# An accumulator split into two tiles, and a last unit computed by halves of its activations

## The chip, the cores and the metric

The kernel runs on one core of a Trainium2 chip. The metric is the device time of one launch in microseconds (us). The core has a matrix engine (PE, TensorE; its weight loads are shown apart as PEld), a vector engine (DVE, VectorE), an activation engine (ACT, ScalarE), GpSimd (POOL) and SyncE (SP), whose queue issues nearly all DMAs here. Each engine works through its own list of instructions in order; between engines there are semaphores, which a framework sets from the tiles that instructions read and write. PE writes its results to PSUM; a bank in this text is a piece of it with 512 fp32 values in each partition, the output of one matmul of 128x512.

## What is computed

The reference chains three parts. A gated linear attention over 3072 tokens of 256 channels comes first; then a feed-forward part with token shift, whose output is gated; then a second feed-forward part:

```python
# first feed-forward part (weights 256x1024, 1024x256, 256x256)
xk = mu_k * x + (1 - mu_k) * x_prev
xr = mu_r * x + (1 - mu_r) * x_prev
k = np.maximum(xk @ w_k, 0.0)
v = k * k @ w_v
x = 1.0 / (1.0 + np.exp(-(xr @ w_r))) * v
# second feed-forward part (weights 256x2048, 2048x256)
h = x @ w_in
return (h - np.tanh(h)) @ w_out
```

The kernel evaluates h - tanh(h) by a polynomial where every |h| is small. It counts the sums of squares that lie under a bound, and only if that count falls short does a branch at the very end compute everything again with the exact function. With the inputs given here it doesn't.

## The kernel before, in words

Tokens are the columns. Both feed-forward parts work on six blocks (`j`) of 512 tokens, with the 256 channels as two halves of 128 partitions (`c`). Each fp32 product is made of three matmuls: the weights and the activations are split into a high and a low part, and high x high, low x high and high x low are added up. The first part takes 4 units (`i`) of 256 hidden channels per block, the second 8 units, 48 in all. A unit has an up product into a pair of banks (`product`, lines 755 to 758), elementwise work on ACT and DVE, and a down product (`down_part`, lines 760 to 767: for each `c` three matmuls of 128x512) into the accumulator.

The accumulator `acc` (line 223) is one tile of two banks, `acc[:, c]` for channel half `c`. It has one buffer. In the first part, when a block's down products are all in, `final` (line 816) multiplies the whole of it by the gate on DVE, one operation of 128x1024, into `xall`. In the second part two copies (`out_copy`, line 910), one for each `c`, take it to SBUF, and SP stores them. Only then can the down products of the next block begin. Attention takes 12 groups of 256 tokens, which are interleaved with the first feed-forward part up to about 165 us; weights are decoded on the way. PE also writes `acc` in the prologue: matmuls on zeros that fill waiting time, and one small product (lines 217, 562, 659 to 666).

The order of the instructions of each engine isn't written out by hand. `Plan` (line 108) is a list scheduler that runs when the program is built: each step is a task with an estimated time on one or two possible engines (`t_dve(n)` is (n + 145)/960 us, `t_act` the same for ACT), with what it comes after, a rank, and the buffers (`Ring`) that it takes. `run` always issues the task that can start first by these estimates, by rank where several can, and chooses the engine where a task may run on two. `final` is such a task, with `t_dve(1024)` = 1.218 us. The real start is set by the semaphores, not by the estimates.

The last of the 48 units has its elementwise work cut into two halves (`x`, the two blocks of 128 hidden channels), so that each operation is 128x512: square with its sum (`poly_a`), `poly_b`, `poly_c`, `g_high`, `g_low`. Behind the plan, `count` (line 955) compares the 49 columns of sums with the bound on DVE, adds them up over the partitions with a matmul into `pv`, and writes `flag`. Then `last_unit` (line 962) does the last down products in three parts of the output: (`c` 0, 512 columns), (`c` 1, first 256), (`c` 1, last 256), each over both halves of the activations, 18 matmuls; it loads `flag` into registers of every engine, and copies the three parts with ACT, DVE, ACT in turn, with a store behind each. After that comes the branch over the second computation (line 1040).

Of the kernel before, what the change touches and what calls it, by code (L numbers as in the profile page):

```python
# [69 lines left out]
def t_act(n, more=0.0):  # L70
    return 0.172 + n / 1200 + more


def t_dve(n):
    return (n + 145) / 960
# [32 lines left out]
class Plan:  # L108
# [10 lines left out]
    def add(self, on, fn, after=(), rank=0.0, takes=(), uses=(), port=False, dma=0.0, func=None):  # L119
        t = Task()  # L120
        t.on, t.fn, t.rank, t.takes, t.port, t.dma, t.func, t.end = on, fn, rank, takes, port, dma, func, None
        t.after = [x for x in after if x is not None]
        for ring, key in (*takes, *uses):
            ring.use(key, t)
        self.tasks.append(t)
        return t
# [69 lines left out]
def chain_kernel(ctx, tc, xb, a, an, a0, bc, mu_k, mu_r, w_k, w_v, w_r, w_in, w_out, out):  # L196
# [17 lines left out]
    def fill(n):  # L214

        for _ in range(n):
            PE.matmul(acc[:, 0], quiet, quiet.unsqueeze(1).to_broadcast([P, NC4, P]), start=True, stop=True)

    def bank(name, shape=(2, BLK)):
        return pairs.tile([P, *shape], F32, tag="pair", name=name)  # L220


    acc = accp.tile([P, 2, BLK], F32, name="acc")


    WORK = dict(xh=2, xl=2, l=3, h=3, f=3, s=2)
# [23 lines left out]
    def block(j, o):  # L250

        c, n = col(j * BLK) + o, col(j * BLK + GT) - col(j * BLK)
        return xall[:, :, c:c + 2 * n].rearrange("p c (h s) -> p c h s", s=n)[..., 0:GT]

    def halves(t):
        return t.rearrange("p c (h s) -> p c h s", s=GT)
# [294 lines left out]
    def prologue(fetch1):  # L551
# [7 lines left out]

        def warm(n):  # L560
            for _ in range(n):
                PE.matmul(acc[:, 0], quiet, quiet.unsqueeze(1).to_broadcast([P, NC4, P]), start=True, stop=True)

        def load(t, v):
            return lambda: nc.sync.dma_start(out=t, in_=v)
# [92 lines left out]

        def t_dec():

            ps = acc[:, 1]
            for i in range(2):
                PE.matmul(ps[:, 0:NU], tri, las[:, i], start=i == 0, stop=i == 1)

        def t_dexp():
            A.activation(out=dec.rearrange("p g q c -> p (g q c)"), in_=acc[:, 1, 0:NU], func=AF.Exp)

        def t_nu():
            for nm in "kr":
# [90 lines left out]
    def down_part(wh, wl, hl, k, e, first, last):  # L760

        h, l = hl
        for c in range(2):
            cs = slice(c * P, (c + 1) * P)
            PE.matmul(acc[:, c], wh[:, k, cs], h[:, e], start=first, stop=False, skip_group_check=True)  # L765
            PE.matmul(acc[:, c], wl[:, k, cs], h[:, e], start=False, stop=False, skip_group_check=True)  # L766
            PE.matmul(acc[:, c], wh[:, k, cs], l[:, e], start=False, stop=last, skip_group_check=True)  # L767

    mixes, mixed, gate, prs, pks, kks, ksq = ({} for _ in range(7))

# [43 lines left out]
            V.tensor_tensor(out=kk, in0=kk, in1=kk, op=ALU.mult)  # L814

    def final(j):
        V.tensor_tensor(out=block(j, 0), in0=halves(acc), in1=halves(gate.pop(j)), op=ALU.mult)  # L817

    MM6 = 6 * 0.23

    def ffn1(X, wk, wr, wv):

        fin, began = {}, {}
        for j in range(NBLK):
            r0 = RANK_F0 + RANK_F * j
            need = [X.get(i) for i in range(2 * j - 1, 2 * j + 2)]
            mx = {}
            for nm, r in (("k", r0 - 3), ("r", r0 + RANK_R - 3)):
                x, fm = (R["x"], (nm, j)), (R["f"], (nm, j))
                m = add(dict(A=2 * t_act(BLK)), lambda e, nm=nm, j=j: mix(nm, j), [*need, began.get((j - 1, 1 if nm == "k" else NP - 1))], r - 0.1, [fm])  # L830
                m = add(dict(V=2 * t_dve(BLK)), lambda e, nm=nm, j=j: mix_ahead(nm, j), [m], r, (), [fm], port=True)
                h = add(dict(A=t_act(1024), V=t_dve2(1024)), lambda e, q=(nm, j): high(e, mixed, q, mixes[q], "xh"), [m], r, [x], [fm], port=True)
                mx[nm] = add(dict(V=t_dve(1024)), lambda e, q=(nm, j): low(mixed, q, mixes[q], "xl"), [h], r, (), [x, fm], port=True)
            p = mx["r"]
            for m in range(2):
                p = add(dict(P=MM6), lambda e, j=j, m=m: receptance(j, m), [p, wr], r0 + RANK_R, [] if m else [(R["pair"], ("pr", j)), (R["s"], ("rs", j))], [(R["x"], ("r", j))])
            rs = add(dict(A=t_act(1024)), lambda e, j=j: sigmoid(j), [p], r0 + RANK_R, (), [(R["pair"], ("pr", j)), (R["s"], ("rs", j))], func="sig")
            dn = None
            for i in range(NP):
                r = r0 + RANK_U * i  # L840
                pair, fk, l, h = ((R[x], ("k", j, i)) for x in ("pair", "f", "l", "h"))
                p = mx["k"]
                for e2 in range(2):
                    p = add(dict(P=MM6), lambda e, j=j, i=i, e2=e2: up(j, i, e2), [p, wk[i]], r, [] if e2 else [pair, fk], [(R["x"], ("k", j))])
                last_up = began[j, i] = p
                q = add(dict(A=t_act(1024), V=t_dve(1024)), lambda e, j=j, i=i: relu(j, i, e), [p], r, (), [pair, fk])
                q = add(dict(A=t_act(1024), V=t_dve(1024)), lambda e, j=j, i=i: square(j, i, e), [q], r, (), [fk], port=True)
                q = add(dict(A=t_act(1024), V=t_dve2(1024)), lambda e, q=(j, i): high(e, ksq, q, kks[q], "h"), [q], r, [h], [fk], port=True)
                q = add(dict(V=t_dve(1024)), lambda e, q=(j, i): low(ksq, q, kks[q], "l"), [q], r, [l], [fk, h], port=True)
                for e2 in range(2):  # L850
                    k = 2 * i + e2
                    dn = add(
                        dict(P=MM6), lambda e, j=j, i=i, e2=e2, k=k: down_part(wvh, wvl, ksq[j, i], k, e2, k == 0, k == 2 * NP - 1),
                        [q, dn, wv[i]], r + RANK_D, [] if k else [(R["acc"], ("f1", j))], [l, h],
                    )
            fin[j] = add(dict(V=t_dve(1024)), lambda e, j=j: final(j), [dn, rs], r0, (), [(R["acc"], ("f1", j)), (R["s"], ("rs", j))])
        return fin, last_up, mx["r"]


# [49 lines left out]

    def out_copy(j, c, e):  # L910
        ob = obs[j, c] = w2["ob"].tile([P, BLK], F32, tag="ob", bufs=3, name="ob")
        copy(e, ob, acc[:, c])

    def out_store(j, c):
        nc.sync.dma_start(out=out[c * P:(c + 1) * P, j * BLK:(j + 1) * BLK], in_=obs[j, c])
# [1 line left out]
    def ffn2(fin, last_up, last_mix, win, wout):  # L917
        ups, last_high = [last_mix] * 2, None
        for j in range(NBLK):
# [5 lines left out]
            for i in range(NP2):  # L925
# [9 lines left out]
                for x in range(2) if end else [0]:  # L935
                    sl = slice(x, x + 1) if end else ALL
                    w = BLK if end else 2 * BLK

                    q = add(dict(A=2 * t_act(w) + 0.2), lambda e, j=j, i=i, sl=sl, c=n + x: poly_a(j, i, sl, c), [p], r, (), [pair, s, fq])
                    q = add(dict(V=t_dve(w)), lambda e, j=j, i=i, sl=sl: poly_b(j, i, sl), [q], r, (), [s, fq], port=True)  # L940
                    q = add(dict(V=t_dve(w)), lambda e, j=j, i=i, sl=sl: poly_c(j, i, sl), [q], r, (), [pair, fq])
                    q = last_high = add(dict(A=t_act(w), V=t_dve2(w)), lambda e, j=j, i=i, sl=sl: g_high(j, i, sl, e), [q, last_high], r, [] if x else [h, l], [fq], port=True)
                    q = add(dict(V=t_dve(w)), lambda e, j=j, i=i, sl=sl: g_low(j, i, sl), [q], r, (), [l, h, fq], port=True)
                    gl.append(q)
                if end:
                    break
                for e2 in range(2):
# [4 lines left out]
                    q = add(dict(A=t_act(BLK), V=t_dve(BLK)), lambda e, j=j, c=c: out_copy(j, c, e), [dn], r, [ob], [(R["acc"], ("f2", j))])  # L952
                    add(dict(S=0.38), lambda e, j=j, c=c: out_store(j, c), [q], r, (), [ob], dma=0.7)

    def count():

        V.tensor_scalar(out=less, in0=sums, scalar1=T2, scalar2=0.0, op0=ALU.is_lt, op1=ALU.add, accum_out=w2["okc"])
        pv = bank("pv")
        PE.matmul(pv[0:1, 0, 0:1], w2["okc"], ones, start=True, stop=True)
        V.tensor_copy(flag, pv[0:1, 0, 0:1])  # L960

    def last_unit():

        j, i = NBLK - 1, NP2 - 1
        h, l = gs[j, i]
        parts = [(0, slice(0, BLK)), (1, slice(0, GT)), (1, slice(GT, BLK))]
        for c, t in parts:
            cs = slice(c * P, (c + 1) * P)
            for e in range(2):
                wh, wl = (w2["out" + x][i][:, e, cs] for x in "hl")  # L970
                for w, g in ((wh, h), (wl, h), (wh, l)):
                    PE.matmul(acc[:, c, t], w, g[:, e, t], start=False, stop=e == 1 and g is l, skip_group_check=True)
        below = nc.values_load(flag[0:1, 0:1], min_val=0, max_val=P * (NU2 + 1))
        for (c, t), e in zip(parts, "AVA"):
            ob = w2["ob"].tile([P, BLK], F32, tag="ob", bufs=3, name="ob")
            copy(e, ob[:, t], acc[:, c, t])
            nc.sync.dma_start(out=out[c * P:(c + 1) * P, j * BLK + t.start:j * BLK + t.stop], in_=ob[:, t])
        return below

# [26 lines left out]
    with tc.manual_schedule():  # L1006
# [26 lines left out]
            done2.append(decode(100 + n, lambda n=n: unit_jobs(n // 2)[n % 2], lambda: w2["ob"], "2", RANK_X0 + RANK_X * n, [op]))  # L1033
        ffn2(fin, last_up, last_mix, done2[0::2], done2[1::2])
        plan.run()
        count()
        below = last_unit()
        w1_stack.close()
        again = ctx.enter_context(tc.tile_pool(name="again", bufs=1))
# [65 lines left out]
```

## Time and profile before

| | us |
|---|---|
| median of 3 runs | 507.31 (507.01 to 508.74) |
| the profiled execution | 507.41 |
| its span, first to last instruction | 505.7 |

| engine | busy us | share of the span |
|---|---|---|
| PE | 482.5 | 95% |
| DVE | 401.4 | 79% |
| ACT | 293.1 | 58% |
| POOL | 6.1 | 1% |

A busy time is a sum of durations of single instructions. Matmuls overlap in the records: one of 128x512 is shown with some 0.39 us, but in a run of them one starts every 0.23 us. What PE loses is therefore read best from the starts: where two that follow one another are further apart than 0.23 us, PE waited.

### The profile page before, as it was taken

How to read it: one execution, taken by the hardware profiler on the slowest of the kernel's cores; microseconds unless marked ns; L12 is line 12 of the kernel's file. 1: busy time of each engine (PE TensorE's matmuls, PEld its weight loads, DVE VectorE, ACT ScalarE, POOL GpSimd, SP SyncE). 2: the span in 40 equal slices, each digit the busy share in tenths (PEclk: the TensorE clock that was granted, in tenths of full speed). 3: DMA queues.
4: the chain of work that ended last, by engine and by line, in shares of the span. 5: the costliest groups of instructions: out<-in, count | busy, mean ns of one | idle time of the engine just before them, and what ended most of it. 6: DMA issues, size and time to landing. Idle time of an engine off the chain costs nothing.

```text
span 505.7 us, 10270 instructions
## 1 busy us (share of the span) xinstructions
PE 482.5 (95%) x4462; PEld 382.3 (76%) x4462; DVE 401.4 (79%) x509; ACT 293.1 (58%) x374; POOL 6.1 (1%) x22
## 2 busy tenths in 40 slices
PE   5979989999999999999999999999999999999993
PEld 2557767888778878877788788788878888887882
DVE  6698998999669999996877868767876966787581
ACT  5366976775757666766464654645565454455551
POOL 4000000000000000000000000000000000000000
PEclk9789999999999999999999999999999999999998
DMA  6575455211022212210000100100010010001001
GB/s 196 183 231 181 136 156 152 76 47 34 1 86 84 83 43 84 83 43 0 1 0 1 41 0 1 41 3 0 1 41 0 1 41 1 0 1 41 0 2 47
DMA packets 14259, 27.40 MB, mean 54 GB/s; under 512 B 2392, under 2 KB 3288, under 8 KB 14208
## 3 DMA queue, kind: packets, MB, share of 16 engines
q1 hardware_dynamic: 14140, 26.66, 16.9%
q8 instruction: 37, 0.61, 0.5%
q14 instruction: 14, 0.11, 0.1%
q10 hardware_dynamic: 68, 0.02, 0.0%
HBM read 23.30 MB, written 3.34 MB: 53 GB/s over the span
## 4 chain that ended last, share of the span: by engine, by line
PE 69%; DVE 18%; ACT 6%; DMA 3%; issue 2%; ACTq 0%; POOL 0%; DVEq 0%; POOLq 0%; SPq 0%
PE acc L765 10%; PE acc L767 10%; PE acc L766 10%; PE ph L755 8%; PE ph L758 8%; PE ph L756 8%; PE pk L755 3%; PE pk L756 2%; PE pk L758 2%; DVE l L788 2%; DVE f L889 2%; DVE f L893 1%; DMA raw<-in_w_in 1%; PE py L504 1%; PE py L482 1%
## 5 line engine op out<-in xcount | busy, mean ns | idle before, releaser
L884 ACT ACTIVATE s<-ph 128x1024 f32<-128x1024 f32 (+1 forms) x49 | 49.4, 1009 | 76.3 <-PE ph L758 76.3
L889 DVE SCALAR_TENSOR_TENSOR f<-f,s 128x1024 f32<-128x1024 f32 (+1 forms) x49 | 58.8, 1200 | 34.8 <-ACT f L885 34.4
L755 PE MATMUL ph<-xh,winh 128*128 128x512 f32 x192 | 76.2, 397 | 0.0
L756 PE MATMUL ph<-xh,winl 128*128 128x512 f32 x192 | 75.5, 393 | 0.0
L765 PE MATMUL acc<-h,wouth 128*128 128x512 f32 x188 | 74.5, 396 | 0.2
L767 PE MATMUL acc<-l,wouth 128*128 128x512 f32 x188 | 74.5, 396 | 0.1
L766 PE MATMUL acc<-h,woutl 128*128 128x512 f32 x188 | 74.3, 395 | 0.0
L902 DVE TENSOR_TENSOR l<-f,h 128x1024 fp32r<-128x1024 f32 (+1 forms) x49 | 58.9, 1201 | 18.6 <-ACT h L352 18.0
L352 ACT ACTIVATE h<-f 128x1024 fp32r<-128x1024 f32 (+1 forms) x43 | 44.7, 1039 | 48.5 <-DVE f L893 45.6
L893 DVE TENSOR_TENSOR f<-ph,f 128x1024 f32<-128x1024 f32 (+1 forms) x49 | 58.9, 1201 | 3.3
L758 PE MATMUL ph<-xl,winh 128*128 128x512 f32 x192 | 60.2, 395 | 0.0
L885 ACT ACTIVATE f<-s,biases 128x1024 f32<-128x1024 f32 (+1 forms) x49 | 55.6, 1136 | 1.6
L765 PEld LDWEIGHTS acc<-h,wouth 128*128 128x128 f32 x188 | 35.4, 188 | 10.0 <-ACT f L885 1.4
L755 PEld LDWEIGHTS ph<-xh,winh 128*128 128x128 f32 x192 | 36.1, 188 | 8.8
L758 PEld LDWEIGHTS ph<-xl,winh 128*128 128x128 f32 x192 | 36.1, 188 | 8.6
L767 PEld LDWEIGHTS acc<-l,wouth 128*128 128x128 f32 x188 | 35.4, 188 | 9.2 <-DVE l L902 1.0
L756 PEld LDWEIGHTS ph<-xh,winl 128*128 128x128 f32 x192 | 36.1, 188 | 8.1
L766 PEld LDWEIGHTS acc<-h,woutl 128*128 128x128 f32 x188 | 35.4, 188 | 8.2
L755 PE MATMUL pk<-xh,wkh 128*128 128x512 f32 x96 | 39.3, 409 | 0.0
L765 PE MATMUL acc<-h,wvh 128*128 128x512 f32 x96 | 38.5, 401 | 0.9 <-DVE xall L817 0.9
L756 PE MATMUL pk<-xh,wkl 128*128 128x512 f32 x96 | 38.2, 398 | 0.0
L767 PE MATMUL acc<-l,wvh 128*128 128x512 f32 x96 | 37.6, 392 | 0.3 <-DVE l L788 0.3
(138 smaller groups left out, 754.0 us busy)
## 6 DMA issues: line engine op xcount, KB each, us to landing
bct<-in_bc SPq DMA_DIRECT2D x12, 384.0 KB
xbt<-in_xb SPq DMA_DIRECT2D x12, 384.0 KB
raw<-in_w_in SPq DMA_DIRECT2D x8, 512.0 KB
raw<-in_w_out SPq DMA_DIRECT2D x8, 512.0 KB
out<-ob SPq DMA_DIRECT2D x11, 256.0 KB
raw<-in_w_k SPq DMA_DIRECT2D x4, 512.0 KB
raw<-in_w_v SPq DMA_DIRECT2D x4, 512.0 KB
raw<-in_w_r SPq DMA_DIRECT2D x1, 512.0 KB
```

What stands on the lines that cost most here:

```text
L352: A.activation(out=out, in_=in_, func=AF.Copy)
L755: PE.matmul(o, wh[:, k, ms], hi[:, k], start=k == 0, stop=False)
L756: PE.matmul(o, wl[:, k, ms], hi[:, k], start=False, stop=False)
L758: PE.matmul(o, wh[:, k, ms], lo[:, k], start=False, stop=k == 1)
L765: PE.matmul(acc[:, c], wh[:, k, cs], h[:, e], start=first, stop=False, skip_group_check=True)
L766: PE.matmul(acc[:, c], wl[:, k, cs], h[:, e], start=False, stop=False, skip_group_check=True)
L767: PE.matmul(acc[:, c], wh[:, k, cs], l[:, e], start=False, stop=last, skip_group_check=True)
L884: A.activation(out=s, in_=phs[j, i][:, e], func=AF.Square, accum_out=sums[:, c:c + 1])
L885: A.activation(out=qs[j, i][:, e], in_=s, func=AF.Square, scale=PA, bias=pbias)
L889: V.scalar_tensor_tensor(out=q, in0=q, scalar=PG, in1=s, op0=ALU.add, op1=ALU.mult)
L893: V.tensor_tensor(out=q, in0=phs[j, i][:, e], in1=q, op=ALU.mult)
L902: V.tensor_tensor(out=l[:, e], in0=qs[j, i][:, e], in1=f(h[:, e]), op=ALU.subtract)
```

## The change

`acc` becomes two tiles of one bank, `accs[0]` and `accs[1]`, in the same pool; each use names its own. `final` becomes two operations of 128x512, and its estimate in the plan two times `t_dve(512)`, 1.369 us. Counting becomes a task of the plan, after the squares of the second half of the last unit, at a rank two below its neighbours. `last_unit` first issues the small matmul on the count, then the down products by halves of the activations: all of half 0 (both `c`), then all of half 1, 12 matmuls of 512 columns; the flag is converted behind them in the text. The last copies are `c` 0 whole on DVE, and `c` 1 by halves on ACT.

```diff
-    acc = accp.tile([P, 2, BLK], F32, name="acc")
+    accs = [accp.tile([P, BLK], F32, name=f"acc{c}") for c in range(2)]
...
-            PE.matmul(acc[:, c], wh[:, k, cs], h[:, e], start=first, stop=False, skip_group_check=True)
-            PE.matmul(acc[:, c], wl[:, k, cs], h[:, e], start=False, stop=False, skip_group_check=True)
-            PE.matmul(acc[:, c], wh[:, k, cs], l[:, e], start=False, stop=last, skip_group_check=True)
+            PE.matmul(accs[c], wh[:, k, cs], h[:, e], start=first, stop=False, skip_group_check=True)
+            PE.matmul(accs[c], wl[:, k, cs], h[:, e], start=False, stop=False, skip_group_check=True)
+            PE.matmul(accs[c], wh[:, k, cs], l[:, e], start=False, stop=last, skip_group_check=True)
...
     def final(j):
-        V.tensor_tensor(out=block(j, 0), in0=halves(acc), in1=halves(gate.pop(j)), op=ALU.mult)
+        o, g = block(j, 0), halves(gate.pop(j))
+        for c in range(2):
+            V.tensor_tensor(out=o[:, c], in0=accs[c].rearrange("p (h s) -> p h s", s=GT), in1=g[:, c], op=ALU.mult)
...
-            fin[j] = add(dict(V=t_dve(1024)), lambda e, j=j: final(j), ...
+            fin[j] = add(dict(V=2 * t_dve(BLK)), lambda e, j=j: final(j), ...
...
-        copy(e, ob, acc[:, c])
+        copy(e, ob, accs[c])
...
-                    q = add(dict(A=2 * t_act(w) + 0.2), lambda e, ...: poly_a(j, i, sl, c), ...
+                    q = polys = add(dict(A=2 * t_act(w) + 0.2), lambda e, ...: poly_a(j, i, sl, c), ...
...
+                    if x:
+                        add(dict(V=0.28), lambda e: counted(), [polys], r - 2)
...
-    def count():
+    def counted():

         V.tensor_scalar(out=less, in0=sums, scalar1=T2, scalar2=0.0, op0=ALU.is_lt, op1=ALU.add, accum_out=w2["okc"])
-        pv = bank("pv")
-        PE.matmul(pv[0:1, 0, 0:1], w2["okc"], ones, start=True, stop=True)
-        V.tensor_copy(flag, pv[0:1, 0, 0:1])

     def last_unit():

         j, i = NBLK - 1, NP2 - 1
         h, l = gs[j, i]
-        parts = [(0, slice(0, BLK)), (1, slice(0, GT)), (1, slice(GT, BLK))]
-        for c, t in parts:
-            cs = slice(c * P, (c + 1) * P)
-            for e in range(2):
+        pv = bank("pv")
+        PE.matmul(pv[0:1, 0, 0:1], w2["okc"], ones, start=True, stop=True)
+        for e in range(2):
+            for c in range(2):
+                cs = slice(c * P, (c + 1) * P)
                 wh, wl = (w2["out" + x][i][:, e, cs] for x in "hl")
                 for w, g in ((wh, h), (wl, h), (wh, l)):
-                    PE.matmul(acc[:, c, t], w, g[:, e, t], start=False, stop=e == 1 and g is l, skip_group_check=True)
+                    PE.matmul(accs[c], w, g[:, e], start=False, stop=e == 1 and g is l, skip_group_check=True)
+        V.tensor_copy(flag, pv[0:1, 0, 0:1])
         below = nc.values_load(flag[0:1, 0:1], min_val=0, max_val=P * (NU2 + 1))
-        for (c, t), e in zip(parts, "AVA"):
+        for c, e, t in ((0, "V", slice(0, BLK)), (1, "A", slice(0, GT)), (1, "A", slice(GT, BLK))):
             ob = w2["ob"].tile([P, BLK], F32, tag="ob", bufs=3, name="ob")
-            copy(e, ob[:, t], acc[:, c, t])
+            copy(e, ob[:, t], accs[c][:, t])
             nc.sync.dma_start(out=out[c * P:(c + 1) * P, j * BLK + t.start:j * BLK + t.stop], in_=ob[:, t])
         return below
...
         plan.run()
-        count()
         below = last_unit()
```

The remaining lines of the diff put `accs[0]` or `accs[1]` for `acc[:, 0]` or `acc[:, 1]` in the prologue.

## Rows read from the trace of the kernel before

**Rows 1.** Windows: span of each stretch, then each engine's busy time and count

```profile
core 0: us, PE busy (x) PEld busy (x) DVE busy (x) ACT busy (x) POOL busy (x), PEclk, DMA share, GB/s
85.00:165.00 80.00, 79.77 (x1259) 64.67 (x1246) 69.88 (x99) 54.30 (x66) 0.00 (x0) 1.00 0.20 60
165.00:235.00 70.00, 68.87 (x303) 56.19 (x302) 64.19 (x87) 44.29 (x53) 0.00 (x0) 1.00 0.20 61
235.00:494.00 259.00, 258.68 (x1107) 207.32 (x1105) 195.02 (x179) 137.55 (x177) 0.00 (x0) 1.00 0.03 11
```

**Rows 2.** Timeline, PE in the last unit: start us, us, what [idle before <-releaser]

```profile
493.74 0.39 PE L767 MATMUL acc<-l,wouth 128*128 128x512 f32 x1
495.00 0.19 PE L959 MATMUL pv<-ones,okc 128*1 128x1 f32 x2 [0.87 <-DVE less L957]
495.12 0.50 PE L972 MATMUL acc<-h,wouth 128*128 128x512 f32 x1
495.46 0.39 PE L972 MATMUL acc<-h,woutl 128*128 128x512 f32 x1
...
497.91 0.28 PE L972 MATMUL acc<-l,wouth 128*128 128x256 f32 x1
```

**Rows 3.** Timeline, ACT and DVE in the last unit, up to the count

```profile
493.26 1.48 DVE L902 TENSOR_TENSOR l<-f,h 128x512 fp32r<-128x512 f32 x2
493.37 0.63 ACT L352 ACTIVATE h<-f 128x512 fp32r<-128x512 f32 x1 [0.69 <-DVE f L893]
...
494.65 0.20 DVE L957 TENSOR_SCALAR_CACHE_REDUCE less<-sums 128x49 f32<-128x49 f32 x1
```

**Rows 4.** Timeline, the last copies and the three stores

```profile
498.23 0.60 ACT L352 ACTIVATE ob<-acc 128x512 f32<-128x512 f32 x1 [4.22 <-PE acc L972]
...
498.85 1.31 SPq L977 DMA_DIRECT2D out<-ob  x3
498.86 0.42 DVE L354 COPY ob<-acc 128x256 f32<-128x256 f32 x1 [3.48 <-ACT ob L352]
499.31 0.38 ACT L352 ACTIVATE ob<-acc 128x256 f32<-128x256 f32 x1 [0.49 <-DVE ob L354]
```

**Rows 5.** Instructions of line 1040: xcount, ns min/median/max, first and last start

```profile
L1040 SPq EVENT_SEMAPHORE  x8: 17/17/17, 503.3 to 503.8; - x8
...
L1040 PEldq COMPARE_BRANCH  x1: 3362/3362/3362, 496.0 to 496.0; - x1
...
L1040 SPq COMPARE_BRANCH  x1: 50/50/50, 500.2 to 500.2; - x1
```

**Rows 6.** Timeline, two block boundaries of the second part

```profile
279.48 1.29 DVE L354 COPY ob<-acc 128x512 f32<-128x512 f32 x2 [2.53 <-PE acc L767]
...
280.21 0.63 PE L758 MATMUL ph<-xl,winh 128*128 128x512 f32 x2
280.92 0.47 PE L765 MATMUL acc<-h,wouth 128*128 128x512 f32 x1
281.22 0.39 PE L766 MATMUL acc<-h,woutl 128*128 128x512 f32 x1
...
325.69 0.44 PE L765 MATMUL acc<-h,wouth 128*128 128x512 f32 x1
325.96 0.40 PE L766 MATMUL acc<-h,woutl 128*128 128x512 f32 x1
```

**Rows 7.** Timeline, the fourth block boundary of the first part

```profile
185.50 0.61 PE L758 MATMUL pk<-xl,wkh 128*128 128x512 f32 x2
185.61 1.22 DVE L817 TENSOR_TENSOR xall<-acc,s 128x1024 f32<-128x1024 f32 x1
...
186.98 0.47 PE L765 MATMUL acc<-h,wvh 128*128 128x512 f32 x1 [0.86 <-DVE xall L817]
```

**Rows 8.** Windows, two stretches while attention is still interleaved

```profile
72.00:74.00 2.00, 0.40 (x15) 0.31 (x15) 2.00 (x5) 0.67 (x1) 0.00 (x0) 1.00 0.09 25
74.00:76.00 2.00, 2.00 (x6) 1.57 (x7) 2.00 (x4) 1.58 (x2) 0.00 (x0) 0.56 0.79 208
```

More of the change, by code (lines that the diff above doesn't have):

```diff
@@ L216, in fill @@
         for _ in range(n):
-            PE.matmul(acc[:, 0], quiet, quiet.unsqueeze(1).to_broadcast([P, NC4, P]), start=True, stop=True)
+            PE.matmul(accs[0], quiet, quiet.unsqueeze(1).to_broadcast([P, NC4, P]), start=True, stop=True)
     def bank(name, shape=(2, BLK)):
         return pairs.tile([P, *shape], F32, tag="pair", name=name)
-    acc = accp.tile([P, 2, BLK], F32, name="acc")
+    accs = [accp.tile([P, BLK], F32, name=f"acc{c}") for c in range(2)]
     WORK = dict(xh=2, xl=2, l=3, h=3, f=3, s=2)
@@ L561, in warm @@
             for _ in range(n):
-                PE.matmul(acc[:, 0], quiet, quiet.unsqueeze(1).to_broadcast([P, NC4, P]), start=True, stop=True)
+                PE.matmul(accs[0], quiet, quiet.unsqueeze(1).to_broadcast([P, NC4, P]), start=True, stop=True)
         def load(t, v):
@@ L659, in t_dec @@
         def t_dec():
-            ps = acc[:, 1]
+            ps = accs[1]
             for i in range(2):
@@ L665, in t_dexp @@
         def t_dexp():
-            A.activation(out=dec.rearrange("p g q c -> p (g q c)"), in_=acc[:, 1, 0:NU], func=AF.Exp)
+            A.activation(out=dec.rearrange("p g q c -> p (g q c)"), in_=accs[1][:, 0:NU], func=AF.Exp)
         def t_nu():
@@ L855, in ffn1 @@
                     )
-            fin[j] = add(dict(V=t_dve(1024)), lambda e, j=j: final(j), [dn, rs], r0, (), [(R["acc"], ("f1", j)), (R["s"], ("rs", j))])
+            fin[j] = add(dict(V=2 * t_dve(BLK)), lambda e, j=j: final(j), [dn, rs], r0, (), [(R["acc"], ("f1", j)), (R["s"], ("rs", j))])
         return fin, last_up, mx["r"]
@@ L937, in ffn2 @@
                     w = BLK if end else 2 * BLK
-                    q = add(dict(A=2 * t_act(w) + 0.2), lambda e, j=j, i=i, sl=sl, c=n + x: poly_a(j, i, sl, c), [p], r, (), [pair, s, fq])
+                    q = polys = add(dict(A=2 * t_act(w) + 0.2), lambda e, j=j, i=i, sl=sl, c=n + x: poly_a(j, i, sl, c), [p], r, (), [pair, s, fq])
                     q = add(dict(V=t_dve(w)), lambda e, j=j, i=i, sl=sl: poly_b(j, i, sl), [q], r, (), [s, fq], port=True)
```

## The prediction

> **What bounds the kernel.** I read the windows first. From 85 to 494 us PE does nothing but its own work: it is busy for 79.77 of 80 us, 68.87 of 70 and 258.68 of 259, at the full clock, while DVE has 10.12, 5.8 and 64 us to spare [rows 1]. So in these 409 us only what makes PE start a matmul late costs time, and the changed kernel has the same columns to multiply. The other place is the end. PE's last matmul begins at 497.91 [rows 2], yet the span ends at 505.7: copies, stores and the end of the program stand one behind another there. Second I looked along PE's starts for gaps over 0.23 us (between 85 and 494 they are few), and third at the timeline of the last unit. One word on size: 0.3% of 507.31 is 1.5 us, about what a measurement of this kernel can tell from no change.
>
> **The last unit, PE.** PE has nothing to wait for until 493.74, the start of its last matmul in the plan; the next could start at 493.97. It starts at 495.00, and it is the one on the count: that matmul waits for DVE's comparison at 494.65 [rows 2, 3], which stands on DVE behind both `g_low`. In the changed kernel the comparison lies further up on DVE, and the matmul can go at 493.97: 1.03 us. The first down product follows 0.12 us later, as now, at 494.09. Now the second comes 0.34 after the first, as after any wait, against 0.23 in a run [rows 2]: another 0.11. The columns are the same, 6 x 512 and 12 x 256 against 12 x 512. The last of 12 then starts at 494.09 + 11 x 0.233 = 496.66 and takes 0.39: PE ends at 497.05 instead of 498.19, **1.14 us** earlier.
>
> Are the activations there? Half 0 is needed whole at the third matmul, 494.56; its low part is the first of two from 493.26, done by about 494.0. Half 1 is needed from 494.09 + 6 x 0.233 = 495.49, its low part at 495.96; they are done at 494.00 and 494.74 [rows 3]. The comparison, moved ahead of them on DVE, delays them by its 0.20 us at most: cover of 0.36, 1.29 and 1.02 us is left. If the comparison is put behind them by the plan, the first 1.03 us are not won. I don't expect it: its rank is two lower than that of the steps that become ready with it, and the list scheduler takes the lower. The conversion of the flag comes behind the last `g_low` on DVE, at about 494.95, and the load of the flag on SP still ends a microsecond before SP's first store. `last_unit`'s DVE copy stands behind it in the queue, with the same cover.
>
> **The last copies.** Now ACT reads `c` 0 from 498.23, when all 18 matmuls are done, though the matmuls of `c` 0 are the first six; DVE waits for ACT, ACT again for DVE [rows 4]. All three take turns, 498.23 to 499.69. In the changed kernel `c` 0 ends with the ninth of 12 matmuls: start 495.95, end 496.34. DVE's copy of 512 columns takes at most 0.7 (two take 1.29 [rows 6]): done at 497.05. ACT copies the halves of `c` 1 from 497.07, 0.38 each [rows 4]: done at 497.45 and 497.83. SP needs 1.31 us for three issues [rows 4], some 0.46 from one to the next, so the stores are issued at 497.08, 497.54 and 498.0; now they are at 498.85, 499.3 and 499.77. From there on nothing is changed: SP's branch at 500.2, and its first step behind it at 503.3 [rows 5]. The end is **1.77 us** earlier, PE's 1.14 among them.
>
> Rows 4 show that readers of two different banks take turns here. [...] By the rows alone, if they went on taking turns, it would be 1.2 us; that is a rival below.
>
> **The boundaries of blocks in the second part.** The first down product of a block needs the accumulator free of both copies. At 280.21 PE begins two matmuls, so the next is due at 280.68 and the one after it at 280.91; that one starts at 281.22, 0.31 late. Where ACT copies, at 325.69, the next is 0.27 behind, 0.04 late [rows 6]. There are three boundaries of the first kind and two of the second: 3 x 0.31 + 2 x 0.04 = **1.0 us**. With two tiles the copy of `c` 0 can start 0.70 us sooner (three matmuls of 0.233), and PE needs only `accs[0]` at first and `accs[1]` three matmuls later. Both are free by 280.2, with at least 0.5 us over: all of it goes, and PE, which bounds this stretch, keeps it.
>
> **The boundaries in the first part.** `final` of block 3 starts at 185.61 and PE, due at 185.97, starts at 186.98, some 0.15 behind its end [rows 7]. Its first half would be done at 186.30 and PE could start at 186.45: **0.5 us**. The second half is done by 187.0, before PE's fourth matmul at 187.15. At the other boundaries of this part PE has no gap to give back.
>
> **What it adds.** Two operations of half the size instead of one: 1.29 us for two copies of 512 columns [rows 6] against 1.22 for `final` whole [rows 7], 0.07 us on DVE, six times. PE hides it, being bound; without that cover it costs 0.4 us in all. [...]
>
> **The order.** The estimate of `final` grows by 0.151 us in the plan. From the first `final` at about 93 us on, every later choice on DVE may fall otherwise: which of two ready steps goes first, and whether ACT or DVE takes one. No row shows the new order. With today's order PE stands idle for 0.23 us of 80 between 85 and 165 [rows 1]; an order that happens to be better gives at most that back. A worse one can cost a wait as at 186.98, 0.86 us [rows 7], at several places: 2.5 us for three. I take 0.2 us of loss, near to the low end, since PE has had buffers enough to stay fed and 0.15 us is less than what the estimates are off anyway.
>
> **The sum.** 1.77 + 1.0 + 0.5 - 0.2 = 3.1 us off the profiled execution's 507.41 (its span 505.7, and 1.7 outside it): 504.3. The median of the runs is 0.1 below the profiled one: **504.2 us**.
>
> **The rivals.** *The new order loses some* (0.17): the gains are there, but PE meets new waits of 0.7 to 2.5 us between 93 and 235, where DVE has the least to spare [rows 1]: 504.9 to 506.7.
>
> *The accumulators stay coupled* (0.08): the readers of the two tiles still wait for each other and for the last matmul. Then DVE's copy runs 497.07 to 497.77, ACT's to 498.53, and the third store is issued at about 498.55, 1.2 us sooner than now; nothing is won at the boundaries: 507.3 - 1.2 = 506.1. For it speaks that ACT and DVE do take turns now [rows 4], against it that they now share one tile.
>
> *The end is held by something else* (0.08): SP's first step after the branch is 3.1 us behind it, and PE's branch takes 3.36 us with no store near [rows 5]. If that time grows when several branches and stores fall closer together, up to 1.0 us of the 1.77 is lost: 505.2. Against it: the stores keep their distances to one another and to SP's branch.
>
> *Slower, by the order and the clock* (0.07). [...]
>
> **How the numbers follow.** The forecast has 0.60, with 503.2 to 504.9 as its own range: 503.2 if the order costs nothing, the first-part wait goes whole and ACT's copies overlap a little; 504.9 if the order costs 0.9. The range is 503.2 to 506.2: it takes in the forecast, two thirds of the first rival, the coupled accumulators and the held end, and leaves out some 0.15. Faster means under 505.8: the forecast, the held end, and about half of the first rival, 0.77. Within 0.3%: the rest of it and the coupled accumulators, 0.16. Slower 0.07.
>
> **What would show it.** In the changed kernel's timeline: the small matmul directly behind the plan's last, the comparison on DVE before the last `poly_c`; 12 matmuls 0.23 apart without a gap; DVE's copy running before PE has ended; stores some 0.46 apart, and the same 5.9 us from the third issue to the end. At the five boundaries matmuls 0.23 apart, and the first copy 0.7 us ahead of the second's input. DVE in two halves for each `final`, and PE less than 0.5 us late behind the fourth. The prediction is wrong if PE's busy time from 85 to 235 falls short of the stretch by more than 2 us, if the copies still take turns, or if the third store's issue moves and the end doesn't follow.

## The result, and the profile after

The changed kernel takes 509.79 us (median; 506.04 to 511.84), the kernel before, run beside it, 505.62 (20 runs of each; the 507.31 that the prediction started from is the median of 3). The ratio is **1.0066** [1.0045, 1.0087]: by it the change is slower by 3.3 us (the two medians lie 4.2 apart) where 3.1 us of gain were forecast. The profiled execution took 508.56, its span 506.8.

First the windows, in the columns of [rows 1]:

```profile
core 0: us, PE busy (x) PEld busy (x) DVE busy (x) ACT busy (x) POOL busy (x), PEclk, DMA share, GB/s
85.00:165.00 80.00, 79.77 (x1241) 64.58 (x1224) 69.09 (x101) 55.35 (x67) 0.00 (x0) 1.00 0.19 59
165.00:235.00 70.00, 68.30 (x298) 55.27 (x296) 65.73 (x90) 43.99 (x54) 0.00 (x0) 1.00 0.19 61
235.00:494.00 259.00, 256.35 (x1098) 206.26 (x1098) 193.68 (x181) 134.37 (x173) 0.00 (x0) 1.00 0.03 11
```

Between 85 and 494 us PE was idle for 1.68 us before; now it is for 4.58. PE still bounds the stretch, so this is where the time went. What PE waited for, from 85 to 500 us (total us, times, longest):

```profile
PE acc L767 <- DVE l L904: 2.3, 2, 1.7
PE acc L765 <- ACT h L352: 1.4, 1, 1.4
PE acc L765 <- DVE h L354: 0.6, 1, 0.6
PE py L482 <- DVE f L807: 0.2, 1, 0.2
```

Before, PE waited 0.9 us for the count, 0.9 for `final` [rows 2, 7], and 0.3 and 0.2 elsewhere; only the last line is among these. The timeline shows two places, the first down product of the second part and the last but one unit:

```profile
234.03 0.50 PE L765 MATMUL acc<-h,wouth 128*128 128x512 f32 x1 [1.45 <-ACT h L352]
...
235.29 0.50 PE L767 MATMUL acc<-l,wouth 128*128 128x512 f32 x1 [0.53 <-DVE l L904]
...
491.62 0.50 PE L765 MATMUL acc<-h,wouth 128*128 128x512 f32 x1 [0.58 <-DVE h L354]
491.95 0.40 PE L766 MATMUL acc<-h,woutl 128*128 128x512 f32 x1
494.08 0.50 PE L767 MATMUL acc<-l,wouth 128*128 128x512 f32 x1 [1.73 <-DVE l L904]
...
496.60 0.19 PE L968 MATMUL pv<-ones,okc 128*1 128x1 f32 x2
496.72 0.50 PE L974 MATMUL acc<-h,wouth 128*128 128x512 f32 x1
497.05 0.39 PE L974 MATMUL acc<-h,woutl 128*128 128x512 f32 x1
...
499.38 0.39 PE L974 MATMUL acc<-l,wouth 128*128 128x512 f32 x1
```

The first lines of both places, in the kernel before:

```profile
235.41 0.39 PE L765 MATMUL acc<-h,wouth 128*128 128x512 f32 x1
...
236.08 0.50 PE L767 MATMUL acc<-l,wouth 128*128 128x512 f32 x1
...
491.17 0.40 PE L765 MATMUL acc<-h,wouth 128*128 128x512 f32 x1
...
491.63 0.40 PE L767 MATMUL acc<-l,wouth 128*128 128x512 f32 x1
```

That is 1.98 + 2.31 = 4.29 us of waiting that neither [rows 1] nor the matmuls before [rows 2] have. The wait that [rows 2] show, 0.87 on the count, is gone: `pv` follows the plan's last matmul (496.28) by 0.32. So is the wait of [rows 7]; there `final` now has two halves, and PE goes on between them:

```profile
185.00 1.28 DVE L819 TENSOR_TENSOR xall<-acc,s 128x512 f32<-128x512 f32 x2
185.20 0.61 PE L758 MATMUL pk<-xl,wkh 128*128 128x512 f32 x2
185.80 0.19 PEld L765 LDWEIGHTS acc<-h,wvh 128*128 128x128 f32 x1 [0.41 <-ACT s L801]
185.83 0.47 PE L765 MATMUL acc<-h,wvh 128*128 128x512 f32 x1
```

The end, against [rows 4] and [rows 5]:

```profile
499.12 0.69 DVE L354 COPY ob<-acc 128x512 f32<-128x512 f32 x1 [2.15 <-PE acc L974]
499.81 0.66 ACT L352 ACTIVATE ob<-acc 128x256 f32<-128x256 f32 x2 [4.52 <-DVE ob L354]
499.84 1.83 SPq L980 DMA_DIRECT2D out<-ob  x3
```

DVE's copy begins while PE still runs, so the copies no longer take turns. (ACT's row names DVE's copy because that ends within 0.04 us of PE's last matmul. In e1, a run below, ACT starts at 494.12, 0.04 us behind PE's end at 494.08 and before DVE's copy ends at 494.13.) But the three issues on SP take 1.83 us together where they took 1.31.

### The profile page after: what moved, and what is told of

The parts are those of the page before. It is cut to its first block, busy times and chain, and to the rows that moved or that the text cites. A ratio compares the mean times of both kernels' runs of the same rounds, so it can differ in the third digit from the quotient of the medians.

```text
span 506.8 us, 10267 instructions
## 1 busy us (share of the span) xinstructions
PE 480.3 (95%) x4456; PEld 380.8 (75%) x4456; DVE 402.3 (79%) x515; ACT 291.1 (57%) x374; POOL 6.1 (1%) x22
## 4 chain that ended last, share of the span: by engine, by line
PE 70%; DVE 17%; ACT 7%; issue 2%; DMA 2%; ACTq 0%; POOL 0%; POOLq 0%; DVEq 0%
PE acc L767 10%; PE acc L765 10%; PE acc L766 10%; PE ph L755 8%; PE ph L758 8%; PE ph L756 8%; PE pk L755 2%; PE pk L756 2%; PE pk L758 2%; DVE l L788 2%; DMA raw<-in_w_in 1%; DVE f L807 1%; DVE wd L320 1%; DVE wd L317 1%; PE py L504 1%
## 5 line engine op out<-in xcount | busy, mean ns | idle before, releaser
L767 PE MATMUL acc<-l,wouth 128*128 128x512 f32 x188 | 74.6, 397 | 2.4 <-DVE l L904 2.3
L352 ACT ACTIVATE h<-f 128x1024 fp32r<-128x1024 f32 (+1 forms) x41 | 42.5, 1037 | 50.7 <-DVE f L895 48.1
L767 PEld LDWEIGHTS acc<-l,wouth 128*128 128x128 f32 x188 | 35.3, 188 | 11.9 <-DVE l L904 3.7
L767 PE MATMUL acc<-l,wvh 128*128 128x512 f32 x96 | 37.5, 391 | 0.0
```

The source lines that it names most:

```text
L352: A.activation(out=out, in_=in_, func=AF.Copy)
L767: PE.matmul(accs[c], wh[:, k, cs], l[:, e], start=False, stop=last, skip_group_check=True)
```

## The experiments

Up to the first `final` all these kernels have the same order, yet that stretch differs from one execution to the next by up to 3.9 us (first `final` at 90.15 to 94.06). So in the table PE's time is counted from the first `final` to the end of its last matmul ("PE"). "Waits" are PE's idle times over 0.05 us after 100 us, added up; "tail" runs from the last matmul's start to the end of the span. All are from one profiled execution each; the ratio is from the timed runs against the kernel before on the same chip. The profiled executions of e4, e6, e10 and e11 took 1.8 to 3.5 us more than the medians of their timed runs, so what they show need not be in most of those runs.

| kernel | estimate of `final` | ratio | PE | waits | tail |
|---|---|---|---|---|---|
| before | 1.218 | 1 | 404.86 | 2.47 | 7.77 |
| changed | 1.369 | 1.0066 [1.0045, 1.0087] | 406.74 | 4.65 | 7.45 |
| changed, again (e7) | 1.369 | 1.0058 [1.0037, 1.0080] | 408.43 | 4.72 | 7.73 |
| e1 | 1.218 | 0.9953 [0.9935, 0.9971] | 402.41 | 0.96 | 8.04 |
| e2 | before, with 1.369 | 1.0081 [1.0051, 1.0112] | 407.36 | 4.84 | 7.78 |
| e6 | 1.369 in one block only | 1.0043 [1.0020, 1.0067] | 407.86 | 3.98 | 8.07 |
| e3 | 1.218, tiles only | 0.9958 [0.9942, 0.9974] | 403.90 | 2.16 | 7.31 |
| e4 | 1.218, last unit only | 0.9976 [0.9958, 0.9994] | 403.72 | 1.52 | 6.92 |
| e8 | e1 without branch | 0.9869 [0.9850, 0.9889] | 402.95 | 1.01 | 4.53 |
| e9 | before without branch | 0.9927 [0.9900, 0.9954] | 404.73 | 2.42 | 4.96 |
| e10 | 1.38 | 0.9987 [0.9960, 1.0013] | 407.42 | 3.85 | 6.31 |
| e11 | 1.24 | 1.0015 [0.9982, 1.0048] | 409.10 | 3.98 | 7.43 |
| e12 | 1.25 | 0.9938 [0.9916, 0.9961] | 401.80 | 0.47 | 7.35 |
| e5 | 1.45 | 0.9889 [0.9872, 0.9905] | 401.46 | 0.44 | 6.56 |

**Is it the estimate?** One run undoes the estimate alone in the changed kernel.

```diff
-            fin[j] = add(dict(V=2 * t_dve(BLK)), ...
+            fin[j] = add(dict(V=t_dve(1024)), ...
```

> The changed kernel with one number put back: final's estimate in the plan is 1.218 us again, so that the order of PE, ACT and DVE is that of the kernel before up to the last unit. Theory A (the new order costs it all; tiles and tail bring what was predicted): 3.1 to 3.6 us below the kernel before, ratio 0.993; PE's starts at the five boundaries of the second part 0.23 us apart, the third store's issue about 1.8 us earlier behind PE's last planned matmul. Theory B (two tiles, two halves of final or the tail themselves cost): it stays 2 to 4 us above the kernel before, as the changed kernel does.

The other makes it alone, in the kernel before.

```diff
-            fin[j] = add(dict(V=t_dve(1024)), ...
+            fin[j] = add(dict(V=2 * t_dve(BLK)), ...
```

> The kernel before with one number changed: final's estimate is 2 x t_dve(512) = 1.369 us; what is computed and how is as before, only the order differs. Theory A: slower than the kernel before by what the changed kernel lost and what it gained besides, 3.3 + 3.3, so 5 to 8 us, ratio 1.010 to 1.016, with PE waiting for h and l at the start of the second part and ahead of the last unit. Theory B: within 0.3% of the kernel before.

The estimate alone makes the kernel before slower by 0.81%, less than the 1.0 to 1.6% expected; the change without it makes it faster by 0.47%, 2.4 us, less than the 3.1 to 3.6 expected (where the rest stayed is told with the prediction below). What e1's PE waits for from 85 to 500 us is little:

```profile
PE acc L767 <- DVE l L788: 0.5, 1, 0.5
PE py L482 <- DVE f L807: 0.2, 1, 0.2
PE acc L765 <- ACT s L801: 0.2, 1, 0.2
```

The loss is thus the order that the plan draws up, not the new tiles, halves or copies.

**The parts by themselves**, both with the old estimate and so with the old order. e3 leaves the last unit, the count and the copies as they were:

```diff
-        for e in range(2):
-            for c in range(2):
-                cs = slice(c * P, (c + 1) * P)
...
+        parts = [(0, slice(0, BLK)), (1, slice(0, GT)), (1, slice(GT, BLK))]
+        for c, t in parts:
...
+        count()
```

> The kernel before with the accumulator as two tiles and final in two halves; the estimate and the tail of the kernel before, so PE's order is the same throughout. Theory A: 1.3 to 1.7 us faster in the boundaries (0.31 us at three of them, 0.04 at two, 0.5 at the fourth boundary of the first part) and 0.2 to 0.6 more at the end, since the copy of channel half 0 need not wait for half 1. Theory B: 1 us or more slower, the halves of final lengthening DVE.

e4 takes those from the change and keeps one tile and `final` whole:

```diff
-    accs = [accp.tile([P, BLK], F32, name=f"acc{c}") for c in range(2)]
+    acc = accp.tile([P, 2, BLK], F32, name="acc")
+    accs = [acc[:, c] for c in range(2)]
...
-        for c in range(2):
-            V.tensor_tensor(out=o[:, c], in0=accs[c]..., in1=g[:, c], op=ALU.mult)
+        V.tensor_tensor(out=block(j, 0), in0=halves(acc), in1=halves(gate.pop(j)), op=ALU.mult)
```

> The kernel before with the last unit of the change (count in the plan, halves of the activations, copies DVE, ACT, ACT), but the accumulator one tile and the old estimate. Theory A: PE ends 1.1 us earlier, but the three copies still take turns, some 1.5 us as before: 1.1 us faster, ratio 0.998. Theory B (the count in the plan holds DVE up in the last unit): no gain or up to 2 us slower.

Each is faster than the kernel before. PE's time falls by 0.96 and 1.14 us, and by 2.45 with both (e1); the timed ratios of e1 and e3 can't be told apart. In e3 PE is 1.27 us ahead behind the last block boundary, just under the 1.3 to 1.7 expected; then it waits 1.2 us for the count, 0.3 longer than before.

**Where does the order go wrong?** e6 gives the larger estimate to one of the six `final`, e7 is the changed kernel once more.

```diff
-            fin[j] = add(dict(V=2 * t_dve(BLK)), ...
+            fin[j] = add(dict(V=2 * t_dve(BLK) if j == 2 else t_dve(1024)), ...
```

> The changed kernel with the old estimate in five blocks and the new one, 0.151 us more, in block 2 alone. By the scheduler PE's order is that of the changed kernel. Theory A: as slow as the changed kernel, 2 to 4 us above the kernel before, with PE's two waits at the start of the second part (1.4 and 0.5 us) and ahead of the last unit (some 2 us). Rival (the loss grows with the number of lengthened tasks): a sixth of it, 0.5 us above the run with the old estimate everywhere.

> The changed kernel again, unchanged, beside the others on the same chip, for a second profile. Theory A: 3 to 4 us above the kernel before; from the first final to the end 1.5 to 4 us more than the kernel before took there (412.4 us), with the same waits in the same places. Rival (the first profile was a lucky one and something before the first final is slower as well): the stretch up to the first final longer than the 90.6 to 94.1 us of the other profiles.

e6 is about as slow as the changed kernel, so the loss doesn't grow with the number of lengthened tasks. Both have the two waits at the end (0.58 and 1.73 in e7); at the start e6's first wait is 0.20 us where 1.4 were expected. In both something comes on top that the first profile lacks: the clock (PE's time less its waits is 403.9 us in e6 and 403.7 in e7, 402.1 in the first profile). e7's timeline, and a window in the columns of the first fence:

```profile
490.61 0.50 PE L765 MATMUL acc<-h,wouth 128*128 128x512 f32 x1 [0.58 <-DVE h L354]
...
493.07 0.79 PE L767 MATMUL acc<-l,wouth 128*128 128x512 f32 x1 [1.73 <-DVE l L904]
493.66 0.63 PE L765 MATMUL acc<-h,wouth 128*128 128x512 f32 x1
494.09 0.63 PE L766 MATMUL acc<-h,woutl 128*128 128x512 f32 x1
```

```profile
493.00:496.00 3.00, 2.93 (x7) 2.35 (x8) 1.90 (x4) 0.63 (x1) 0.00 (x0) 0.50 0.00 0
```

Behind the waits the granted clock is 0.50 (in the first profile 1.00, also from 493 to 496 us); a matmul starts every 0.43 us there and not every 0.23. From the same matmul (L767 behind the wait) to `pv` it takes 4.02 us, in the first profile 2.52: 1.5 us more.

The order can be read from the lists of instructions. The kernel before, e1, e5 and e12 have the first line of each pair, the changed kernel, e2, e6 (there every instruction of PE stands as in the changed kernel) and e11 the second (half an up product is 6 matmuls, 1.4 us; units of the whole second part, 0 to 47):

```
start   up 1, up 2, up 1, up 2, down 0 (whole), up 3 ...
        up 1, up 2, up 1, down 0, up 2, down 0, up 3 ...
end     up 46, down 43, up 46, down 44, up 47, down 44, up 47, down 45, down 46, pv
        up 46, down 43, up 47, down 44, up 46, down 44, up 47, down 45, down 46, pv
```

At the start the first down product now stands half an up product earlier in PE's list, and PE comes to it before ACT has written its activations. At the end the second half of unit 46's up product has changed places with the first half of unit 47's. (The two lists also differ between 203 and 228 us and once at each of the five block boundaries of the second part; in the changed kernel PE doesn't wait there.) ACT shows it: unit 46's square (128x1024) and unit 47's first (128x512), in e1 and then in the changed kernel:

```profile
479.82 1.03 ACT L886 ACTIVATE s<-ph 128x1024 f32<-128x1024 f32 x1 [3.30 <-PE ph L758]
...
486.25 0.58 ACT L886 ACTIVATE s<-ph 128x512 f32<-128x512 f32 x1
```

```profile
485.48 1.03 ACT L886 ACTIVATE s<-ph 128x1024 f32<-128x1024 f32 x1 [2.22 <-PE ph L758]
...
488.28 0.60 ACT L886 ACTIVATE s<-ph 128x512 f32<-128x512 f32 x1 [0.50 <-PE ph L758]
```

There were 6.4 us between the two units, and 2.8 are left. DVE then has both at once, and unit 46's last step, for which PE waits, stands behind work for unit 47 and behind the count:

```profile
490.88 0.68 DVE L354 CAST h<-f 128x1024 fp32r<-128x1024 f32 x1
491.48 0.20 DVE L961 TENSOR_SCALAR_CACHE_REDUCE less<-sums 128x49 f32<-128x49 f32 x1
...
491.60 0.68 DVE L891 SCALAR_TENSOR_TENSOR f<-f,s 128x512 f32<-128x512 f32 x1
492.21 0.68 DVE L895 TENSOR_TENSOR f<-ph,f 128x512 f32<-128x512 f32 x1
492.81 1.21 DVE L904 TENSOR_TENSOR l<-f,h 128x1024 fp32r<-128x1024 f32 x1
```

**Is a larger estimate bad, or PE's order?** Four other values separate the two. 1.24 gives the changed kernel's order of PE at both places; 1.25 and 1.45 give PE's old order to the instruction, up to the last unit; 1.38 has yet another start (unit 0's first down product sooner still) and the old end.

```diff
-            fin[j] = add(dict(V=2 * t_dve(BLK)), ...
+            fin[j] = add(dict(V=1.24), ...
```

> The change with the estimate of final at 1.24, 0.02 above the old one. By the lists of instructions PE has the changed kernel's order at the start of the second part and in the last units, though the estimate is nearer to the old one than the changed kernel's is. Theory, 'PE's order at these two places decides': waits of about 1.4 and 0.5 us at 232 to 236, of about 0.6 and 1.7 at 491 to 494; 508 to 510 us, 1.004 to 1.009 of the kernel before. Rival, 'the size of the estimate or other places on DVE and ACT decide': near the change with the old estimate, 502 to 504, 0.994 to 0.997.

> The change with the estimate of final at 1.25, 0.01 above the run with 1.24. By the lists of instructions PE's order is here that of the kernel before everywhere but in the last unit's own matmuls, the same as in the runs with 1.218 and 1.45; DVE and ACT have an order of their own. Theory, 'PE's order decides': no wait of PE above 0.6 us after the first final, full clock to PE's end, PE from the first final to its end 401 to 403 us; 500 to 503.5 us, 0.988 to 0.996 of the kernel before. Rival, 'the estimate's nearness decides, so that 1.25 behaves as 1.24': 506 to 507.5, 1.000 to 1.004.

> The change with the estimate of final at 1.38 instead of 1.369. By the lists of instructions its second part begins with yet another order on PE (unit 0's down product comes before unit 2's up product, sooner still than in the changed kernel), but its last units stand as in the kernel before. Theory, 'PE's order decides, and the loss has two places': waits of 2 us or more at 228 to 236 us, none above 0.2 us at 491 to 494, no low clock in the last unit; 505 to 507 us, 0.999 to 1.003 of the kernel before. Rival a, 'the end alone costs (its waits of 2.3 us and the low clock behind them)': 502 to 503.5, as the change with the old estimate. Rival b, 'any larger estimate spoils the order': 508 to 510.

> The changed kernel with the estimate of final raised further, from 1.369 to 1.450 us. By the scheduler PE's order is then that of the kernel before again up to the last unit (DVE's and ACT's differ in places). Theory A (what costs is which order comes out, not how long final is taken to be): like the run with the old estimate, 2 to 3 us below the kernel before, without PE's waits at the start of the second part and ahead of the last unit. Rival (a longer estimate costs by itself, the more the longer): slower than the changed kernel, 4 us or more above the kernel before.

1.24 and 1.25 lie 0.01 us apart and give 1.0015 and 0.9938; 1.45, further up than the changed kernel's, is the fastest of all. So neither size nor nearness decides. No run changes PE's order alone, though: DVE's and ACT's lists differ as well, in e6 and e11 from the changed kernel's and in e5 from e1's from about 104 us on, in e12 from 170. That PE's order at the two places decides is the reading that fits all the runs, and PE's waits there are the direct evidence. PE's waits in e12, 85 to 500 us, are down to the one that all kernels have:

```profile
PE py L482 <- DVE f L807: 0.2, 1, 0.2
```

e11's end has the changed kernel's waits and a longer low clock (timeline, then a window):

```profile
489.65 0.50 PE L765 MATMUL acc<-h,wouth 128*128 128x512 f32 x1 [0.58 <-DVE h L354]
...
492.11 0.79 PE L767 MATMUL acc<-l,wouth 128*128 128x512 f32 x1 [1.72 <-DVE l L904]
```

```profile
492.00:498.00 6.00, 5.89 (x15) 4.25 (x16) 2.09 (x5) 0.63 (x1) 0.00 (x0) 0.50 0.00 0
```

At its start e11 has only 0.20 where 1.4 were expected, and its timed loss is accordingly smaller than forecast (0.15%, and not certain to be one). PE's order alone doesn't fix a wait's length: e6, with the changed kernel's list on PE and other lists on ACT and DVE, has 0.20 there too, and the changed kernel 1.45. e10 has no wait at its end, as expected, and its waits at the start are larger than thought and partly elsewhere (1.16 us at 231 to 233, 2.46 at 242 to 246), with the low clock behind the second (timeline, then a window):

```profile
244.38 0.50 PE L765 MATMUL acc<-h,wouth 128*128 128x512 f32 x1 [1.93 <-ACT h L352]
```

```profile
246.00:249.00 3.00, 3.00 (x8) 2.32 (x8) 2.93 (x4) 0.51 (x1) 0.00 (x0) 0.50 0.00 0
```

Its timed runs are level with the kernel before: what the change gains is lost again, though the end is clean. Rival a is refuted by that, rival b by e12 and e5.

**The tail.** The same last unit, copies and stores give a tail of 6.31 (e10) to 8.07 us (e6). e8 and e9 leave out the branch and the second computation behind it:

```diff
-        again = ctx.enter_context(tc.tile_pool(name="again", bufs=1))
-        with tc.If(below < P * (NU2 + 1)):
-            any_again(again)
```

> The run with the old estimate, with the branch at the end and the second computation behind it left out; the count and the load of the flag stay. Theory T (the fetches of instructions behind the branch and the last stores get in each other's way): SP's three issues 0.46 us apart or as soon as the copies are done, each 0.33 to 0.4 us long instead of up to 1.2, SP's waits at the end 3.3 us or less behind PE's last matmul's start instead of 5.7, and 2 to 3 us less in all than with the branch. Rival (the stores alone set the end): the same distance from PE's last matmul to the end, no gain over 0.5 us.

> The kernel before without the branch at the end and the second computation (both are left out; with these inputs the branch is never entered). Theory, 'the fetches behind the branches lie across the stores whenever the end comes': the time from PE's last matmul's start to the end of the span falls from 7.77 us to about 5.0 (the changed kernel without the branch has 4.53, and here the third store goes 0.5 later, since the copies take turns), and the time falls by 2.8 us against the kernel before, to about 0.9945. Rival, 'the branch costs more only because the copies of the changed kernel come earlier': then here only SP's own branch and its first step are saved, 1 us at most; 0.998 or above, end 6.8 us or more behind PE's last start.

The tail falls by 3.5 us (e1 to e8) and 2.8 (before to e9), the time by 0.8% and 0.7% of the kernel. First e1's stores in the timeline, and the queues from 493 to 502 us (kind: packets, MB, share); then the same of e8, the queues from 488.5 to its end:

```profile
494.15 2.12 SPq L980 DMA_DIRECT2D out<-ob  x3
```

```profile
q1 hardware_dynamic: 432, 0.52, 17.3%
q14 instruction: 5, 0.04, 2.0%
q8 instruction: 2, 0.03, 1.5%
```

```profile
493.55 1.31 SPq L980 DMA_DIRECT2D out<-ob  x3
```

```profile
q1 hardware_dynamic: 432, 0.52, 16.6%
```

Without the branch the three issues take 1.31 us again, and no packets of instructions run beside the stores. The stores' own packets then take 1.6 us from the first to the last (494.38 to 495.97), in e1 3.6 (494.99 to 498.61). In the kernel before the issues take 1.31 us with the branch and without it; its 2.8 us come behind the third issue, from which it is 5.92 us to the end, in e9 3.11; with the branch the stores' packets take 3.2 us. Behind its own branch SP waits 3.1 us in the kernel before and 3.0 in e1; in e9 and e8 it waits 1.5 for the stores instead. That the branch costs this is shown; that it is its instruction packets (7 from 493 to 502 us in e1, none in e8) that slow SP and the stores is only the likeliest reading.

## Why the prediction was wrong

**What bounds the kernel** was read rightly: PE's waits account for the loss, and by and large the kernels sort by them; e10, level with the kernel before in spite of 3.85 us of waits in its profile, is the clearest exception. The sign of being wrong that the prediction set for PE, more than 2 us short between 85 and 235 us, stayed just below, at 0.23 + 1.70 = 1.93, because the second place lies at 491.

**The last unit.** 1.14 us were forecast. PE's order in e1, e5 and e12 is that of before up to the last unit, so each matmul can be set beside its twin; the last unit gains 0.93, 0.92 and 0.93. The missing 0.2: `pv` still goes out 0.32 behind the matmul ahead of it and not 0.23, and the second down product still follows the first by 0.33. The forecast of 0.23 at both places was wrong; what holds PE back there isn't shown.

**The boundaries of the second part.** 1.0 us, forecast 1.0: in e1 the cumulative lead over before grows from 0.51 to 1.52 between 236 and 461 us, in three steps of 0.3 and two near nothing. PE at the boundary of [rows 6], in e1:

```profile
278.08 0.63 PE L758 MATMUL ph<-xl,winh 128*128 128x512 f32 x2
278.55 0.39 PE L765 MATMUL acc<-h,wouth 128*128 128x512 f32 x1
278.78 0.39 PE L766 MATMUL acc<-h,woutl 128*128 128x512 f32 x1
```

0.47 and 0.23 between starts, where it was 0.71 and 0.30. **The fourth boundary of the first part** gave 0.66 (forecast 0.5). e1 then loses 0.32 at 224 us on a low part, which e5 and e12 don't; with 0.17 won at 234 us its PE is ahead by 0.66 - 0.32 + 0.17 + 1.01 + 0.93 = 2.45 us, against 2.64 in the forecast's terms. **What it adds**, 0.07 us for a `final` in two, is 1.28 against 1.22: 0.06, hidden.

**The last copies and stores** were mis-sized. The 1.77 us took for granted that two tiles of one bank end the taking of turns; no row of the kernel before shows that, it was the author's estimate. The runs do show it (DVE's copy at 499.12 runs beside PE's last matmuls, into the other bank), and the rival of coupled accumulators is refuted. With one tile (e4) DVE's copy starts at 497.82, 0.04 behind the end of PE's last matmul, and ACT's at 498.55, behind the end of DVE's; with two (e1) DVE's starts at 493.44, 0.64 before PE's end, and ACT's at 494.12, before DVE's ends. But of 0.63 us behind PE's end (1.77 - 1.14) the undisturbed end gives 0.54 (from the end of PE's last matmul to the end of the span 4.68 in e9, 4.14 in e8), and with the branch, against 7.49 before, anything from a loss of 0.2 (e1, e6) to a gain of 1.6 (e10). What failed there is the assumption that SP keeps 0.46 us from one issue to the next and that nothing changes from the third issue on: SP's three issues took 1.73 (e7) to 2.23 us (e12) where the new copies meet the branch, and the end followed the third issue by 4.4 us (e10) to 6.4 (e6), by 5.9 before. The rival "the end is held by something else" named this mechanism.

**The order** is the step that failed and decided the sign. The sum took 0.2 us of loss for it; the same change with the old order and with the new one differ by 406.74 - 402.41 = 4.3 us of PE's time in the profiles, and by 1.7 more where the clock falls. Two arguments in it failed. The first was that 0.151 us is less than what the estimates are off anyway: in a list scheduler a small difference needn't have a small effect, since one choice made otherwise can change later ones, and 0.01 us (1.24 to 1.25) moved 1.7 us of waiting in one place. The second was that PE has buffers enough. [Rows 1] say the opposite when they are read as a bound: with 1.68 us idle of 409 a new order could win little and lose much. And the end of the plan, where there is no later work to fill in, was not looked at.

The rival nearest to it is the one given 0.07, **slower, by the order and the clock**. In kind it is what happened, at 509.79: four waits of PE (0.53 to 1.73 us, at 232 to 235 and 491 to 494), with a low clock (0.50 in e7) behind them in some executions only; the stretch to 165 is untouched (79.77 busy in both). The loss by the order that the likelier rival allowed, 2.5 us at most between 93 and 235, is met by 1.98 us at 232; the 2.31 at 491 lie outside it.

Two things stay open: why e5 is faster than e12 by half a per cent with the same order of PE (0.34 us of PE and 0.8 of the tail are seen in the profiles, of 2.5), and in how many of the timed runs of the changed kernel the clock fell.

e5, the change with 1.45 as the estimate, beats both kernels: 500.44 us, 0.9889 of the kernel before.

## What to carry to other kernels

An estimate in a list scheduler is a switch between whole orders and not a quantity with a proportional effect: measure a change with the old order held, set the two instruction lists side by side, and choose the order afterwards from several estimates by measured time. Where the bounding engine idles as little as here (1.68 us of 409), take a new order as a risk with a price, and look for it where work runs out: at the seams between parts and at the end. At the end of a kernel, time the stores with what else is fetched at that moment, since a shorter chain of copies may only move into it (e1's tail is 8.04 us, 7.77 before).

## What the chip showed that was not expected

- A branch that isn't meant to be entered costs the end of this kernel 2.8 to 3.5 us, in SP's wait behind the branch (3.1 before, 3.0 in e1) and in slower stores (packets over 3.6 us in e1, 1.6 in e8); in the kernels with the new copies SP's three issues slow down as well (1.73 to 2.23 us, 1.31 in e8 without the branch).
- The clock fell behind PE's waits of 0.58 and 1.73 us in three of the five profiled executions with that end (e6, e7, e11; not in the first of the changed kernel nor in e2), and behind waits of 1.93 and 0.53 in e10. The windows behind the waits show 0.50 in e7, e10 and e11; in e7 the clock had been 1.00 from 85 us on. In the kernels without those waits nothing speaks for such a fall between the first `final` and PE's end: PE's time less its waits is 401.0 to 402.4 us in them, 402.1 and 402.5 in the first of the changed kernel and e2, and 403.6 to 405.1 in e6, e7, e10 and e11.
